# Two passes over the tokens in a kernel of pooled attention and a gated MLP, with Strassen's scheme in the second

## The chip, the cores and the metric

The kernel runs on one core of one Trainium2 chip. A core has five engines that run their own queues of instructions in order: TensorE (PE, matmuls and transposes; its weight loads are shown as PEld), VectorE (DVE), ScalarE (ACT), GpSimd (POOL) and SyncE (SP), which here issues all DMAs. Matmul results land in PSUM, in eight banks of 128 partitions x 512 fp32; everything else is worked on in SBUF. The metric is the device time of one execution in microseconds. Three runs of the kernel before gave 826.31, 827.72 and 828.11 us; the median is 827.72.

## The reference

Inputs are float32 q, k and v, and float64 weights (the kernel reads them as pairs of 32-bit words and makes fp32 numbers of them itself).

```python
# attention: q, k, v are (8 batches, 8 heads, 576 tokens, 64)
k_p = k.reshape(B, H, 72, 8, D).mean(axis=3)       # 8 neighbours pooled
v_p = v.reshape(B, H, 72, 8, D).mean(axis=3)
scores = (1 / sqrt(64)) * (q @ k_p.T)
attn = softmax(scores)                              # over the 72 pooled keys
x = (attn @ v_p) -> (4608 tokens, 512)
# MLP: w1, w2 (512, 1024), w3 (1024, 1024), w_out (1024, 512)
out = ((x @ w1) * (x @ w2)) @ w3 @ w_out            # (4608, 512)
```

## The kernel before

**Numbers.** Each matmul operand is split in two parts, hi + lo, of the type fp32r, and a product is made of three matmuls: hi*hi, hi*lo, lo*hi (`PASSES`, L499). `split` (L153) makes the parts: ACT casts to hi, DVE or POOL subtracts to get lo. A float64 weight becomes fp32 in four instructions: `high` on ACT (L133), `low` on DVE (L138), `conv_b` (L146) and `conv_c` (L150) on DVE.

**Start.** w3 @ w_out is computed once as W, since h @ w_out = g @ (w3 @ w_out). It takes 16 steps s (`w_mm`, L565): eight with the upper half of w3's rows (with w_out converted beside it by `w_block`, L166), eight with the lower half (`w_conv`, `w_conv2`, `w_conv3`, `w_split`, L214 to L227). Each step converts a 512 KB piece of w3, turns it by four PE transposes (`w_turn`, L207), splits it and runs 12 matmuls of 512 columns into four accumulators. `w_post` (L575) splits the result into W's tiles. Then, or beside it, 16 pieces of w1 and w2 are loaded, converted and split (`w12_conv` to `w12_split`, L229 to L248).

**Main loop.** The 4608 tokens go in 12 chunks m of 384. For each of the eight blocks j of 128 columns of w1 and w2, `a_mm` and `b_mm` (through `ab`, L503, matmul L510) compute 12 matmuls of 384 columns each; `a_post` copies a out of PSUM (ACT, L520), `b_post` multiplies (DVE, L530) and casts the product to hi (ACT, L531), `g_lo` makes lo (DVE, L536); `out_mm` (L538, matmul L545) runs nine matmuls of 512 columns (three token tiles, three passes) into `o0`, `o1`, `o2`, which collect over all j. `out_post` copies them out and stores them. The PSUM accumulators `a`, `b`, `o0`, `o1`, `o2` have one bank each.

**Attention** of chunk n is done while chunk n-1 is in the main loop, in three tiles of 128 tokens, or four of 96 where the chunk crosses a batch (n % 3 == 1). For each tile: scores in two halves of four heads (`s_mm`, L389), per half the row minimum, a subtraction, exp and a sum (`soft1`: DVE L405, L407, ACT L410, DVE L411; tiles in `SOFT_ACT` use another form, L415), normalisation (`soft2`, L424 to L427), the eight keys beyond 64 set aside in R (`soft3`, L436, L438), transposes (`pt_mm`, `ptr_mm`, L449, L459), their split (`pt_post`, L471, L472). Then four head pairs of probabilities times v (`av_mm`, L484 to L487), split into x (`av_post`, L495, L496). All attention results on PE share three PSUM buffers named `att`. k and v are pooled by additions on POOL (`pool_tree`, L346; three k pieces by DVE, L304, as listed in `K_DVE`); q is loaded in small pieces (L276) and transposed on DVE (L287).

**Order.** The order is written out by hand: `at(kind, k, fn, ...)` (L584) puts a step into slot k; steps are sorted by slot, within a slot by kind (L loads, P post-processing, M main matmuls, A attention matmuls), and each engine runs its part of that list in order. A main-loop chunk has 24 slots (3 per j): a, b, and at +5 the out group. K0 is the slot after the first eight w3 steps, M0 = K0 + 16 the slot where chunk 0 begins.

Of the kernel before, what the change touches and what calls it, by code (L numbers as in the profile page):

```python
# [29 lines left out]
):  # L30

    nc = tc.nc
# [14 lines left out]
    NK = DM // P  # L49
    CH = 384  # L50
    NCH = NTOK // CH

    SOFT_ACT = [(0, 0), (0, 1), (0, 2), (1, 1), (1, 2)]
    LO_DVE = [(0, 1), (4, 1), (6, 0)]
    K_DVE = [(0, 1), (1, 1), (1, 3)]
# [3 lines left out]
    xp = ctx.enter_context(tc.tile_pool(name="xp", bufs=2))  # L59
    p1 = ctx.enter_context(tc.tile_pool(name="p1", bufs=1))  # L60
    p2 = ctx.enter_context(tc.tile_pool(name="p2", bufs=2))
    stp = ctx.enter_context(tc.tile_pool(name="stp", bufs=4))
    osp = ctx.enter_context(tc.tile_pool(name="osp", bufs=3))
    pacc = ctx.enter_context(tc.tile_pool(name="pacc", bufs=1, space=PSUM))
    patt = ctx.enter_context(tc.tile_pool(name="patt", bufs=3, space=PSUM))


    ident = cp.tile([P, P], F32, name="ident")
    kbd = [cp.tile([P, NPR, 2 * KP], F32, name=f"kbd{i}") for i in range(2)]
    vbd = [[cp.tile([P, NPR, P], F32R, name=f"vbd{i}_{s}") for s in range(2)] for i in range(2)]  # L70
    VR = [cp.tile([P, NPR, P], F32R, name=f"VR{i}") for i in range(2)]
# [41 lines left out]
    def load_wo(j):  # L113
        raw["wo", j] = raw_cell(8 + j)
        nc.sync.dma_start(out=raw["wo", j], in_=wor[j * P:(j + 1) * P, :])

    def load_w3(s):
        h, j = divmod(s, NJ)
        raw["w3", s] = raw_cell(s % 4)
        nc.sync.dma_start(  # L120
            out=raw["w3", s].rearrange("p (i c) -> p i c", i=4),
            in_=w3r[h * 512:(h + 1) * 512, 2 * j * P:2 * (j + 1) * P].rearrange("(i p) c -> p i c", p=P))

    def load_w12(j, w):
# [19 lines left out]
    def conv_b(r, z):  # L144

        nc.vector.scalar_tensor_tensor(  # L146
            out=r, in0=z.bitcast(I32), scalar=3, in1=r, op0=ALU.logical_shift_left, op1=ALU.bitwise_or)

    def conv_c(r, z):
# [7 lines left out]
    def w_tiles(s):  # L157
# [4 lines left out]
        if s < NJ:  # L162
            stage["wo", s] = stage["wt"][s % 4], f(stage["wt"][4 + s % 3])
        stage["w3", s] = W_cell(0, 4 + s % 4, I32), W_cell(1, 4 + s % 4, F32)

    def w_block(v):  # L166
# [47 lines left out]
    def w_conv(s):  # L214
        w_tiles(s)
        conv_a(raw.pop(("w3", s)), *stage["w3", s])

    def w_conv2(s):
        conv_b(*stage["w3", s])

    def w_conv3(s):
        conv_c(*stage["w3", s])

    def w_split(s):
        ps = w_turn(s)
        w3t[s] = hl_cell(4 + s % 4)
        split(ps, *w3t[s])  # L227

    def w12_conv(j, w):  # L229
# [37 lines left out]
    def load_q(n, prs=range(NPR)):  # L267
        if ("q", n) not in stage:
            stage["q", n] = p1.tile([P, NPR, CH // 32, 32], F32, tag="qs", name="qs")
        t = stage["q", n]  # L270
        for pr in prs:
            for (b, s0, cnt, off) in pieces(n):
                for par in range(2):
                    for db in range(2):
                        g = 2 * par + db
                        nc.sync.dma_start(  # L276
                            out=t[32 * g:32 * g + 32, pr, off // 32:(off + cnt) // 32],
# [212 lines left out]
    def av_post(n, pr):  # L490
# [5 lines left out]
        nc.vector.tensor_tensor(out=xl, in0=ps, in1=f(xh), op=ALU.subtract)  # L496


    PASSES = ((0, 0), (0, 1), (1, 0))  # L499
# [38 lines left out]
    def out_mm(m, j):  # L538
# [3 lines left out]
        for t in range(3):  # L542
            c = slice(t * P, (t + 1) * P)
            for i, (sg, sw) in enumerate(PASSES):
                nc.tensor.matmul(out=oacc[m][t], lhsT=(gh, gl)[sg][:, c], rhs=W[j][sw],  # L545
# [189 lines left out]
```

## Time and profile before

| | us |
|---|---|
| median of three runs | 827.72 |
| profiled execution | 828.94 |
| its span, first to last instruction | 827.2 |
| PE busy | 784.6 |
| DVE busy | 460.5 |
| ACT busy | 283.2 |
| POOL busy | 205.7 |
| first main-loop matmul of chunk 0 starts | 107.74 |
| first main-loop matmul of chunk 1 starts | 184.03 |

The span is that of the profiled execution, which took 828.94 us as a whole. Busy times are sums of instruction durations; matmul ends are modelled and overlap the next start, so PE's pace is better read from starts. "Idle before" is the time an engine waited ahead of an instruction, with the instruction or transfer that ended the wait.

### The profile page before, as it was taken

What the parts mean: (1) busy time and instruction counts of PE and PEld (TensorE: products, weight loads), DVE (VectorE), ACT (ScalarE), POOL (GpSimd) and SP (SyncE); (2) the same over time, 40 slices, a digit from 0 to 9 for tenths busy, and PEclk for the clock granted to TensorE, in tenths of its full rate; (3) what the DMA queues carried; (4) which work ended last, traced back from release to release, by engine and by line L of the source; (5) the groups of instructions that cost most, each with busy time, mean ns of one, the idle gap of its engine ahead of it and who ended that gap; (6) DMA issues with size and microseconds to landing.
All of it is one profiled execution on the core that took longest, in us unless ns stands there. A gap on an engine that the chain in (4) does not pass through costs nothing.

```text
span 827.2 us, 11655 instructions
## 1 busy us (share of the span) xinstructions
PE 784.6 (95%) x4320; PEld 727.5 (88%) x4320; DVE 460.5 (56%) x921; ACT 283.2 (34%) x719; POOL 205.7 (25%) x234
## 2 busy tenths in 40 slices
PE   7877697799999999999999999999999999999998
PEld 6655596699999999999999999999999999999997
DVE  7987999937537436446345355365374374462112
ACT  4535555523224223323233234232243233232211
POOL 2152546601600811105104603006008112000000
PEclk8989988999999999999999999999999999999999
DMA  9996893005304402016014330053034030100101
GB/s 328 214 184 158 223 219 73 1 1 123 88 0 90 108 35 56 1 47 151 16 49 86 77 77 1 0 115 97 1 87 111 25 67 1 39 1 1 40 0 39
DMA packets 113161, 62.64 MB, mean 76 GB/s; under 512 B 80208, under 2 KB 96848, under 8 KB 113104
## 3 DMA queue, kind: packets, MB, share of 16 engines
q1 hardware_dynamic: 113104, 61.89, 30.2%
q8 instruction: 34, 0.56, 0.3%
q14 instruction: 23, 0.19, 0.1%
HBM read 52.43 MB, written 9.44 MB: 75 GB/s over the span
## 4 chain that ended last, share of the span: by engine, by line
PE 80%; DVE 10%; DMA 7%; issue 2%; ACT 1%; SPq 0%; DVEq 0%
PE a L510 23%; PE o L545 23%; PE b L510 23%; PE att L389 4%; DMA raw<-in_moe_w_dram 3%; PE att L449 2%; DMA qs<-in_q_dram 2%; PE att L486 1%; PE att L484 1%; PE att L485 1%; PE att L487 1%; DMA raw<-in_moe_w_out_dram 1%; DVE wb L146 1%; PE att L459 1%; DVE wb L138 1%
## 5 line engine op out<-in xcount | busy, mean ns | idle before, releaser
L510 PE MATMUL a<-xT,hl 128*128 128x384 f32 x1152 | 224.1, 343 | 0.0
L510 PE MATMUL b<-xT,hl 128*128 128x384 f32 x1152 | 221.4, 340 | 0.0
L510 PEld LDWEIGHTS a<-xT,hl 128*128 128x128 f32 x1152 | 206.4, 192 | 4.8
L510 PEld LDWEIGHTS b<-xT,hl 128*128 128x128 f32 x1152 | 200.0, 189 | 0.0
L545 PE MATMUL o<-Wc,gh 128*128 128x512 f32 x576 | 183.6, 400 | 0.0
L530 DVE TENSOR_TENSOR a<-b,a 128x384 f32<-128x384 f32 x96 | 53.1, 554 | 125.8 <-PE b L510 125.7
L545 PEld LDWEIGHTS o<-Wc,gh 128*128 128x128 f32 x576 | 105.1, 189 | 17.3
L347 POOL TENSOR_TENSOR st<-st 72x512 f32<-72x512 f32 (+1 forms) x53 | 75.0, 1415 | 175.2 <-DMA st<-in_k_dram 162.4
L545 PE MATMUL o<-Wc,gl 128*128 128x512 f32 x288 | 114.0, 396 | 0.0
L520 ACT COPY a<-a 128x384 f32<-128x384 f32 x96 | 45.9, 479 | 182.8 <-PE a L510 163.6
L531 ACT CAST gh<-a 128x384 fp32r<-128x384 f32 x96 | 49.2, 512 | 149.0 <-DVE a L530 149.0
L536 DVE TENSOR_TENSOR gl<-a,gh 128x384 fp32r<-128x384 f32 x96 | 62.4, 650 | 34.9 <-ACT gh L531 34.5
L360 POOL TENSOR_TENSOR vbd<-vm,vbd 64x256 fp32r<-64x256 f32 x16 | 13.4, 836 | 253.2 <-ACT vbd L359 248.3
L496 DVE TENSOR_TENSOR xT<-att,xT 128x384 fp32r<-128x384 f32 x48 | 26.6, 556 | 70.8 <-ACT xT L495 70.8
L545 PEld LDWEIGHTS o<-Wc,gl 128*128 128x128 f32 x288 | 54.1, 188 | 12.5
L411 DVE TENSOR_REDUCE sm<-E 128x4 f32<-128x288 f32 (+1 forms) x70 | 31.6, 451 | 46.3 <-ACT E L410 46.3
L571 PE MATMUL o<-hl 128*128 128x512 f32 x144 | 45.3, 455 | 11.0 <-DVE hl L179 10.9
L389 PE MATMUL att<-kbd,qT 128*128 128x144 f32 (+1 forms) x320 | 53.3, 290 | 2.0 <-ACT E L415 2.0
L405 DVE TENSOR_REDUCE mx<-att 128x4 f32<-128x288 f32 (+1 forms) x80 | 35.9, 449 | 29.5 <-PE att L389 29.5
L389 PEld LDWEIGHTS att<-kbd,qT 128*128 128x128 f32 (+1 forms) x320 | 47.4, 182 | 3.1 <-ACT E L415 2.5
L410 ACT ACTIVATE E<-E 128x288 f32<-128x288 f32 (+1 forms) x70 | 31.1, 445 | 55.1 <-DVE E L407 55.1
L571 PEld LDWEIGHTS o<-hl 128*128 128x128 f32 x144 | 30.3, 218 | 19.3 <-DVE hl L179 12.9
(87 smaller groups left out, 850.1 us busy)
## 6 DMA issues: line engine op xcount, KB each, us to landing
raw<-in_moe_w_dram SPq DMA_DIRECT2D x32, 512.0 KB
st<-in_k_dram SPq DMA_DIRECT2D x32, 288.0 KB
out_dram<-ob SPq DMA_DIRECT2D x35, 256.0 KB
st<-in_v_dram SPq DMA_DIRECT2D x32, 256.0 KB
qs<-in_q_dram SPq DMA_DIRECT2D x128, 48.0 KB
raw<-in_moe_w_out_dram SPq DMA_DIRECT2D x8, 512.0 KB
st<-in_v_dram SPq DMA_DIRECT2D x64, 64.0 KB
qs<-in_q_dram SPq DMA_DIRECT2D x128, 24.0 KB
```

Of the source, the lines that this page charges most:

```text
L347: nc.gpsimd.tensor_tensor(out=t[:, :, 0:4], in0=t[:, :, 0:4], in1=t[:, :, 4:8], op=ALU.add)
L389: nc.tensor.matmul(out=ps[:nt, 2 * KP * j:2 * KP * (j + 1)], lhsT=qT[n][:, pr, off:off + nt], rhs=kbd[b % 2][:, pr], start=True, stop=True,)
L405: nc.vector.tensor_reduce(out=mx[:nt, hs], in_=sv, axis=AX.X, op=ALU.min)
L410: nc.scalar.activation(out=E[:nt, hs], in_=E[:nt, hs], func=AF.Exp, scale=-1.0)
L411: nc.vector.reduce_sum(out=sm[:nt, hs], in_=E[:nt, hs], axis=AX.X)
L510: nc.tensor.matmul(out=o, lhsT=w12[j, w][sw][:, kt * P:(kt + 1) * P], rhs=x[sx][:, kt], start=(i == 0), stop=(i == 3 * NK - 1))
L520: nc.scalar.copy(out=a, in_=gt[m, j][:, :CH])
L530: nc.vector.tensor_tensor(out=g, in0=ps[:, :CH], in1=g, op=ALU.mult)
L531: nc.scalar.copy(out=gh, in_=g)
L536: nc.vector.tensor_tensor(out=gl, in0=g, in1=f(gh), op=ALU.subtract)
L545: nc.tensor.matmul(out=oacc[m][t], lhsT=(gh, gl)[sg][:, c], rhs=W[j][sw], start=(j == 0 and i == 0), stop=(j == NJ - 1 and i == 2))
L571: nc.tensor.matmul(out=wacc[h][it], lhsT=w3t[s][sa][:, it * P:(it + 1) * P], rhs=wo[j][sb], start=(j == 0 and i == 0), stop=(j == NJ - 1 a ...
```

## The change

The tokens are gone through twice. The first pass is the old loop with four of the eight blocks j (`NA = 4`), so it uses half of w1's and w2's columns and half of W. Its result goes to a scratch tensor in DRAM (`pd`), and x goes there too (`xd`). In the first pass's slots the second half of W is computed in eight units, one a chunk (`w2_load` to `w2_post`), and stored (`wbd`); from chunk 8 on the other half of w1 and w2 is converted, and the sums that Strassen's scheme needs are made and split (`w12b_*`).

The second pass goes through the eight batches of 576 tokens. For each of four groups qq (two of w1, two of w2, each 256 columns by 512 rows), the product of 2 x 2 blocks is made of seven block products instead of eight (Winograd's form): six matmuls of 288 columns each, in one of five accumulators in turn. The sums of x are made once a batch, the sums of the products by DVE adds from PSUM; for w2 POOL multiplies with the w1 result. Then tiles of 128 tokens go through the second half of W, the first pass's partial result is loaded and added, and the sum is stored.

In the start, the w3 steps are eight instead of 16, and the w1/w2 pieces eight instead of 16; M0 is K0 + 8. A chunk has 12 slots. One piece of k goes from DVE to POOL (`K_DVE`), two lo parts of w1/w2 too (`LO_DVE`), q is buffered per head pair, `stp` and `osp` have one buffer less, `out_post` always copies on ACT, and the SBUF pools of the first pass are released for those of the second.

```diff
-    LO_DVE = [(0, 1), (4, 1), (6, 0)]
-    K_DVE = [(0, 1), (1, 1), (1, 3)]
+    LO_DVE = [(0, 1)]
+    K_DVE = [(0, 1), (1, 1)]
...
+    def w2_conv(u):
+        t = cell(11, [P, 2, 512], I32, "wt")
+        stage["w2", u] = t[:, 0], f(t[:, 1])
+        conv_a(raw.pop(("w2", u)), *stage["w2", u])
...
+    def w2_mm(u):
+        ps = stage["w2p", u] = patt.tile([P, 512], F32, tag="att", name="att")
+        t = w3t.pop(("w2", u))
+        for jj in range(4):
+            for i, (sa, sb) in enumerate(PASSES):
+                nc.tensor.matmul(out=ps, lhsT=t[sa][:, jj * P:(jj + 1) * P], rhs=wo[4 * (u % 2) + jj][sb],
+                                 start=(jj == 0 and i == 0), stop=(jj == 3 and i == 2))
...
+    def w12b_sums(qq):
+
+        r0, r1 = (f(stage["vr"][:, jj]) for jj in range(2))
+        a11, a12, a21, a22 = r0[:, :256], r0[:, 256:], r1[:, :256], r1[:, 256:]
+        t = stage["vz"]
+        s1, s2, s3, s4 = (t[:, i, 256 * o:256 * o + 256] for i in range(2) for o in range(2))
+        add(s1, a21, a22)
+        sub(s2, s1, a11)
+        sub(s3, a11, a21)
+        sub(s4, a12, s2)
...
         nc.scalar.copy(out=xh, in_=ps)
-        nc.vector.tensor_tensor(out=xl, in0=ps, in1=f(xh), op=ALU.subtract)
+        sub(xl, ps, f(xh))
+        if n == pr == 0:
+            stage["xs"] = cell(13, [P, 2, CH], F32, "xs")
+        x = stage["xs"][:, pr % 2]
+        nc.scalar.copy(out=x, in_=ps)
+        for (b, s0, cnt, off) in pieces(n):
+            nc.sync.dma_start(out=xd[b][:, pr, s0:s0 + cnt], in_=x[:, off:off + cnt])
...
+    GROUPS = (("A11", "B11"), ("S2", "T2"), ("S1", "T1"), ("S3", "T3"),
+              ("A12", "B21"), ("S4", "B22"), ("A22", "T4"))
...
+    def x_split(i, n):
+        t = (r1, l1)[i % 2]["p"].tile([P, 2, 2, HS], F32R, tag=f"xo{XN.index(n)}", name="xo")
...
+        split(src, *xo[i, n])
...
+    def grp_mm(i, qq, n):
+        wn, xn = GROUPS[n]
+        ps = acc[i, qq, n] = pacc.tile(
+            [P, 512], F32, tag=("a", "b", "o0", "o1", "o2")[(28 * i + 7 * qq + n) % 5], name="ps")
+        w, x = sw[qq, wn], xo[i, xn]
+        for j, (kt, (a, b)) in enumerate((kt, p) for kt in range(2) for p in PASSES):
+            nc.tensor.matmul(out=ps[:, :HS], lhsT=w[a][:, kt * P:(kt + 1) * P], rhs=x[b][:, kt],
+                             start=(j == 0), stop=(j == 5))
+
+    def grp_post(i, qq, n):
...
+            if w2:
+                add(tmp[into], u, o)
+                nc.gpsimd.tensor_tensor(out=d, in0=d, in1=tmp[into], op=ALU.mult)
+            else:
+                add(d, u, o)
...
+            nc.scalar.copy(out=tmp["m1"], in_=o)
+        elif n == 1:
+            add(tmp["u2"], tmp["m1"], o)
...
+    def out2_mm(i, t, half):
...
+                nc.tensor.matmul(
+                    out=oacc["b", no], lhsT=G[no][a][:, j], rhs=W[1, j][b],
+                    start=(j == 0 and n == 0), stop=(j == 3 and n == 2))
...
+        add(ob, part.pop(no), oacc.pop(("b", no)))
+        nc.sync.dma_start(out=out[no * P:(no + 1) * P], in_=ob)
...
-    M0 = F0 + 2 * NS
+    M0 = K0 + 8
+    IA = 3 * NA
+    E0 = M0 + IA * NCH
+    B0 = E0 + 3
+    IB = 25
...
     for n in range(1, NCH):
-        k = M0 + 3 * NJ * (n - 1)
+        k = M0 + IA * (n - 1)
         nt = len(tok_tiles(n))
-        s0, pt, av = (3, 5.5, 20.5) if n == 1 else (0, 6, 17) if nt == 4 else (0, 5, 15)
...
+        plan_att(n, k, *(
+            ([-4, -2, 0, 2], [0, 2, 5, 7], [8, 8.5, 9, 9.5]) if n == 1 else
+            ([-7, -4, -1, 2], [-2, 1, 4, 7], [8, 8.5, 9, 9.5]) if nt == 4 else
+            ([-7, -3, 1], [-2, 2, 6], [7, 8, 8.5, 9])))
...
+        for g in range(28):
+            k = k0 + g / 2 + (0 if g < 7 else 10.5)
+            at("M", k, grp_mm, i, *divmod(g, 7))
+            at("P", k // 1 + 1 + 0.02 * (k % 1), grp_post, i, *divmod(g, 7))
+        x0 = k0 - (12 if i == 0 else 20)
+        at("L", x0 - 3 if i else x0, x_load, i)
...
+            at("M", r0 + 2 * t + h, out2_mm, i, t, h)
```

More of the change, by code (lines that the diff above doesn't have):

```diff
@@ L212, in w_turn, with w12a_conv @@
         return ps
[L214 to L229, printed above, removed]
+    def w12a_conv(j, w):
         i = 2 * j + w
@@ new lines, in w2_post, with load_w12b @@
+    def w2_post(u):
+        it, hf = divmod(u, 2)
+        ps = stage.pop(("w2p", u))
+        if hf == 0:
+            stage["w2s"] = cell(10, [P, 512], F32, "ws")
+            nc.scalar.copy(out=stage["w2s"], in_=ps)
+        else:
+            add(stage["w2s"], stage["w2s"], ps)
+            nc.sync.dma_start(out=wbd[it], in_=stage["w2s"])
+    NAMES = ("A11", "A12", "S1", "S2", "S3", "S4", "A22")
+    OWN = ((0, 1, 2), (3, 4, 5), (6, 7, 8), (9, 10, 11))
+    BOTH = (12, 13)
+    sw = {}
+    def load_w12b(qq, jj):
+        raw["w12b", qq, jj] = (
+            cell(9, [P, 1024], I32, "raw") if qq < 3 else wcell(jj, [P, 1024], I32, "raw"))
+        load_w12(raw["w12b", qq, jj], NA + 2 * (qq // 2) + jj, qq % 2)
@@ new lines, in w12b_split @@
+    def w12b_split(qq, i):
+        src = stage["sums", qq][i]
+        if i < 3:
+            t = cell(OWN[qq][i], [P, 2, 512], F32R, "sw")
+            for o in range(2):
+                c = slice(256 * o, 256 * o + 256)
+                sw[qq, NAMES[2 * i + o]] = t[:, 0, c], t[:, 1, c]
+            split(src, t[:, 0], t[:, 1])
+            return
+        if qq % 2 == 0:
+            stage["both"] = cell(BOTH[qq // 2], [P, 2, 2, 256], F32R, "sw")
+        both = stage["both"][:, :, qq % 2]
+        sw[qq, "A22"] = both[:, 0], both[:, 1]
+        split(src, *sw[qq, "A22"])
@@ L571, in w_mm @@
                 nc.tensor.matmul(
-                    out=wacc[h][it], lhsT=w3t[s][sa][:, it * P:(it + 1) * P], rhs=wo[j][sb],
-                    start=(j == 0 and i == 0), stop=(j == NJ - 1 and i == 2))
-    def w_post(h):
-        for it in range(4):
-            i = 4 * h + it
-            W[i] = [W_cell(x, i, F32R) for x in range(2)]
-            split(wacc[h][it], *W[i])
+                    out=wacc[0][it], lhsT=w3t[s][sa][:, it * P:(it + 1) * P], rhs=wo[s][sb],
+                    start=(s == 0 and i == 0), stop=(s == NJ - 1 and i == 2))
@@ new lines, with xb, x_load, x_sum1 @@
+    XN = ("B11", "T2", "T1", "T3", "B21", "B22", "T4")
+    GROUPS = (("A11", "B11"), ("S2", "T2"), ("S1", "T1"), ("S3", "T3"),
+              ("A12", "B21"), ("S4", "B22"), ("A22", "T4"))
+    x32, xo, acc, tmp, G, part = {}, {}, {}, {}, {}, {}
+    def xb(i, k2, t2):
+        return x32[i][:, 2 * k2:2 * k2 + 2, t2 * HS:(t2 + 1) * HS]
+    def x_load(i):
+        x32[i] = r2["x"].tile([P, NK, S], F32, tag="x32", name="x32")
+        nc.sync.dma_start(out=x32[i], in_=xd[i])
+    def x_sum1(i):
+        t = stage["xs", i] = [r2["x"].tile([P, 2, HS], F32, tag="xs", name="xs") for _ in range(2)]
+        sub(t[0], xb(i, 0, 1), xb(i, 0, 0))
+        sub(t[1], xb(i, 1, 1), t[0])
@@ new lines, in g_rest @@
+    def g_rest(i, odd):
+        no = 9 * (i // 2) + 4
+        if not odd:
+            G[no] = [l1["p"].tile([P, 4, P], F32R, tag=tag, name=tag) for tag in ("ghs", "gls")]
+        for p in range(2):
+            split(G[i, p][:, :, :64] if odd else G[i, p][:, :, S - 64:],
+                  *(x[:, 2 * p:2 * p + 2, 64 * odd:64 * odd + 64] for x in G[no]))
+    def out2_mm(i, t, half):
+        no, _ = out_tiles(i)[t]
+        if half == 0:
+            oacc["b", no] = patt.tile([P, 512], F32, tag="att", name="att")
+        for j in (2 * half, 2 * half + 1):
+            for n, (a, b) in enumerate(PASSES):
+                nc.tensor.matmul(
+                    out=oacc["b", no], lhsT=G[no][a][:, j], rhs=W[1, j][b],
+                    start=(j == 0 and n == 0), stop=(j == 3 and n == 2))
```

379 lines of the change are left out of this document (245 added, 134 removed).

## The prediction

> **What bounds the kernel now.** I read the page first (span, busy times, the slices and the chain), then busy time by stage, then single instructions of PE and DVE in order of time, then the groups by shape.
>
> ```profile
> span 827.2 us, 11655 instructions
> PE 784.6 (95%) x4320; PEld 727.5 (88%) x4320; DVE 460.5 (56%) x921; ACT 283.2 (34%) x719; POOL 205.7 (25%) x234
> PE   7877697799999999999999999999999999999998
> DVE  7987999937537436446345355365374374462112
> PE 80%; DVE 10%; DMA 7%; issue 2%; ACT 1%; SPq 0%; DVEq 0%
> ```
>
> The slices show two regimes: up to about slice 8 (165 us) DVE is full and PE has holes; after it PE is full and DVE is at half. The stages, cut where chunk 0 and chunk 1 start (columns: stage, its length, busy us and count of PE, PEld, DVE, ACT, POOL, clock, DMA share, GB/s):
>
> ```profile
> 0.00:107.70 107.70, 79.72 (x366) 64.68 (x367) 92.37 (x156) 51.76 (x135) 36.21 (x45) 0.88 0.87 227
> 107.70:184.00 76.30, 65.63 (x348) 60.90 (x347) 62.02 (x104) 35.56 (x104) 38.72 (x27) 0.91 0.30 60
> 184.00:823.20 639.20, 639.20 (x3609) 601.90 (x3608) 305.66 (x661) 195.55 (x480) 130.73 (x162) 1.00 0.21 51
> ```
>
> From 184.0 us on PE has no idle time at all. So there the time is the sum of PE's instructions, and only fewer or shorter matmuls help; before it, only less DVE work does. PE's pace comes from starts, since ends are modelled:
>
> ```profile
> 184.03 2.27 PE L510 MATMUL a<-xT,hl 128*128 128x384 f32 x12
> 228.71 2.24 PE L510 MATMUL a<-xT,hl 128*128 128x384 f32 x12
> 230.79 0.34 PE L484 MATMUL att<-PTh,vbd 128*128 128x384 f32 x1
> 233.57 0.62 PE L545 MATMUL o<-Wc,gh 128*128 128x512 f32 x2
> 235.66 2.27 PE L510 MATMUL a<-xT,hl 128*128 128x384 f32 x12
> 242.27 1.92 PE L510 MATMUL a<-xT,hl 128*128 128x384 f32 x10
> 347.17 0.25 PE L484 MATMUL att<-PTh,vbd 128*128 128x192 f32 x1
> 348.03 2.27 PE L510 MATMUL b<-xT,hl 128*128 128x384 f32 x12
> 819.04 4.19 PE o L545 x18
> ```
>
> Twelve matmuls of 384 columns take 230.79-228.71 = 2.08 us, 0.1733 each; the nine of 512 (three tiles, three passes) 235.66-233.57 = 2.09, 0.2322 each. Both are 0.451 to 0.454 ns a column, with no fixed part. The eight of 192 columns take 348.03-347.17 = 0.86, 0.1075 each, not 0.0867: a floor. A chunk takes 242.27-184.03 = 58.24 us. Of it 192 x 0.1733 + 72 x 0.2322 = 50.0 are MLP matmuls, 8.25 attention. Check: 184.0 + 10 chunks x 58.24 + one without attention 50.0 + the two out groups left over from chunk 0 (4.2) = 820.6; PE ends at 823.2. The span is 4.0 longer (last copy and store), the execution 828.94, so 1.7 lie around the span.
>
> **The change, part by part.**
>
> *PE after the start.* A first-pass chunk has 96 x 0.1733 + 36 x 0.2322 = 25.0 us of MLP and keeps its 8.25 of attention: 33.25. The second half of w3 @ w_out, which leaves the start, becomes 96 matmuls of 512 columns (22.3) and 32 transposes, at the floor of 0.1075 (3.4). The second pass has 8 x 28 x 6 = 1344 matmuls of 288 columns and 36 x 12 = 432 of 512. A matmul of 288 columns is not in the trace. Its bounds are the floor, 0.1075, and the 384-column row, 0.1733; since 288 x 0.451 = 0.130 lies above the floor I take 0.130, for 174.7 us, plus 100.3. From the start of chunk 1: 10 x 33.25 + 25.0 + 4.2 + 25.7 + 275.0 = 662.4. The same stretch in the kernel before is 636.7. So Strassen's seven products for eight save 1152 x 0.1733 - 174.7 = 25 us, and the moved w3 half takes 25.7 of it back. On PE alone the steady part wins nothing. What can be won lies before chunk 1.
>
> [...]
>
> *The start.* Before chunk 1 DVE is the limit: 92.4 + 62.0 = 154.4 us in 184. What leaves it is priced by these groups (columns: count, busy us, mean ns, idle before):
>
> ```profile
> L150 DVE SCALAR_TENSOR_TENSOR Wc<-Wc 128x512 int32<-128x512 int32 x16 | 13.8, 863 | 0.3
> L146 DVE SCALAR_TENSOR_TENSOR Wc<-Wc 128x512 int32<-128x512 int32 x16 | 11.7, 731 | 0.1
> L138 DVE TENSOR_SCALAR Wc<-raw 128x512 int32<-128x512 int32 x16 | 8.2, 521 | 2.9 <-DMA raw<-in_moe_w_dram 2.9
> L155 DVE TENSOR_TENSOR hl<-att,hl 128x512 fp32r<-128x512 f32 x8 | 5.4, 679 | 7.1 <-ACT hl L154 7.1
> L155 DVE TENSOR_TENSOR Wc<-o,Wc 128x512 fp32r<-128x512 f32 x6 | 3.8, 678 | 0.0
> L146 DVE SCALAR_TENSOR_TENSOR wb<-wb 128x512 int32<-128x512 int32 x16 | 13.6, 848 | 0.2 <-ACT wb L133 0.2
> L150 DVE SCALAR_TENSOR_TENSOR wb<-wb 128x512 int32<-128x512 int32 x16 | 11.1, 693 | 0.0
> L138 DVE TENSOR_SCALAR wb<-raw 128x512 int32<-128x512 int32 x16 | 11.9, 742 | 0.0
> L304 DVE TENSOR_REDUCE km<-st 72x128 f32<-72x1024 f32 x3 | 5.7, 1910 | 0.0
> ```
>
> Half of the w3 conversions (33.7 / 2) and all eight L155 splits (5.4) go: 22.3. Four splits of the combined W: 4 x 0.68 = 2.7. Half of the w1/w2 conversions: 36.6 / 2 = 18.3. One L304 goes to POOL: 1.9. Four of chunk 0's eight j, at 0.554 + 0.659 (rows below): 4.9. Together 50.1. Against it, attention of chunk 2 now begins in chunk 0, about half a chunk's softmax, 9 us (19.1 a chunk, below). DVE's work before chunk 1 becomes 113 us. At the occupancy of the start so far (92.4 of 107.7 = 0.86) that is 132 us, with no idle time but the first 4 us or so it is 118. I take 124, nearer the lower end, since the idle time late in the kernel before's chunk 0 came from PE's queue of work, which halves; 118 to 136 stay for the range. DMA doesn't bind earlier: 227 GB/s x 107.7 us = 24.4 MB before chunk 0; 16 loads of 512 KB fewer leave 16 MB, 71 us, and by the same DVE sum chunk 0 starts near 82.
>
> *The first pass.* DVE's rows from 184 to 823 us:
>
> ```profile
> L536 DVE TENSOR_TENSOR gl<-a,gh 128x384 fp32r<-128x384 f32 x88 | 58.0, 659 | 33.7 <-ACT gh L531 33.4
> L530 DVE TENSOR_TENSOR a<-b,a 128x384 f32<-128x384 f32 x88 | 48.8, 554 | 120.9 <-PE b L510 120.9
> L407 DVE TENSOR_TENSOR E<-att,mx 128x288 f32<-128x288 f32 x42 | 19.2, 457 | 1.4
> L411 DVE TENSOR_REDUCE sm<-E 128x4 f32<-128x288 f32 x42 | 19.0, 453 | 21.5 <-ACT E L410 21.5
> L472 DVE TENSOR_TENSOR PTl<-att,PTh 128x512 fp32r<-128x512 f32 x21 | 14.5, 690 | 10.0 <-ACT PTh L471 10.0
> L411 DVE TENSOR_REDUCE sm<-E 96x4 f32<-96x288 f32 x24 | 10.8, 449 | 22.7 <-ACT E L410 22.7
> L557 DVE COPY ob<-o 128x512 f32<-128x512 f32 x12 | 8.2, 683 | 1.7 <-PE o L545 1.7
> L472 DVE TENSOR_TENSOR PTl<-att,PTh 128x384 fp32r<-128x384 f32 x12 | 6.6, 554 | 10.7 <-ACT PTh L471 10.7
> ```
>
> Without the MLP rows (106.8) and the copies (8.2, which go to ACT) 190.7 of 305.66 us are attention: 19.1 a chunk. With four j (4.9) and a w3 unit (one conversion at the means above, 2.1, a split 0.68, half an add) that is 27 us. Added to it are waits inside the softmax which stay as long as the order of its steps does: (21.5 + 22.7 + 10.0 + 10.7) / 10 = 6.5 a chunk. So DVE needs 33.5 us where PE needs 33.25 + 3.2 = 36.4, 92% of the time; before, the same sum was some 36 of 58. Two in-order engines so close, coupled by three "att" buffers, will stall each other. Chunk 9 is worse: no w3 unit, but Strassen's weights, each of four groups 2 x (0.85 + 0.69 + 0.74) + 3 splits x 0.68 + five short ones, about 8.7 us; one and a quarter fall in it: 19.1 + 4.9 + 10.9 + 6.5 = 41 against 33, 8 us late. Bounds for all stalls of the pass: 4 (chunk 9, partly caught up) and 40 (every chunk at 39.5). I take 14.
>
> ACT gains the copies of x (48, near 0.5 us) and all stores' copies and stays near 60%. The stores of x add four to eight DMAs a chunk to SP's queue, each behind an ACT copy; the loads of q, k, v queued behind them run 2.6 slots (7 us) ahead of POOL, which hides that. It costs if SP is full:
>
> ```profile
> 252.15 11.65 SPq L276 DMA_DIRECT2D qs<-in_q_dram x24
> ```
>
> At 0.49 us an issue, some 41 issues a chunk are 20 us of 36. Covered.
>
> *The second pass.* For one of eight batches PE has 28 x 6 x 0.130 + 4.5 x 12 x 0.2322 = 34.4 us. DVE has 28 adds at 0.457 (12.8), four sums and seven splits of twice that size (at most 10.1), ten G splits (4.1), 4.5 last adds at 0.69 (3.1): 30 by durations, which overlap in the trace (L407 lasts 0.46, and so on). PE stays ahead as long as five accumulators, 3.9 us of work, cover DVE's bursts. Bounds of the stalls: 0 and 25 (3 a batch); I take 6, nearer the covered side. The join of the passes waits for three ACT copies of chunk 11's accumulators, which the second pass's third to fifth groups reuse; in the 6.
>
> *The end.* After the last product PE waits for its add, the G split, then runs five tiles: 3 us more than before, 7 in all beyond PE's sum.
>
> *Sum.* 124 + 662.4 + 14 + 6 + 7 = 813.4 span, + 1.7 = 815.1 against 828.94 of the profiled execution. That execution is 1.2 above the median of 827.72, so I state **814**.
>
> **The rivals.**
>
> *DVE sets the first pass (slower).* Its price is above: 92% is a mean, and POOL's blocking grows with density:
>
> ```profile
> 382.80 1.44 DVE L536 TENSOR_TENSOR gl<-a,gh 128x384 fp32r<-128x384 f32 x1
> ```
>
> beside the mean of 0.659. If DVE's chunk comes to 38.6 with that and with imperfect order, eight chunks lose 2.2 and chunk 9 and its neighbours 18: 36 instead of 14, **836**. The point: stalls of the pass above 27 us. [...]
>
> *Nothing stalls.* The start takes 118, the first pass loses 4, the second 2: **794**. For it: 92% and 87% are below 100. Against: 15% of DVE idle in the start.
>
> *The second pass follows DVE.* Should the adds wait behind splits that wait for ACT, 3 us a batch: 24 instead of 6, **832**. Against it: the adds depend on PE alone.
>
> [...]
>
> **How the numbers follow.** Forecast 802 to 825: 0.43. Nothing stalls: 0.21. DVE sets the first pass: 0.24. Second pass on DVE: 0.08. Exposed loads: 0.02. More mishaps at once, beyond 850: 0.02. A measurement of this kernel can tell about 0.2% (1.7 us) from no change. Faster than 826.1: 0.43 + 0.21 + 0.03 from the lighter cases of the others = 0.67; within: 0.05; slower: 0.28. The range 790 to 845 leaves out some 0.04 below and 0.12 above.
>
> **What would show it.** Chunk 1 starting at 118 to 136 us; first-pass chunks of 36 to 38 us with PE idle ended by DVE and ACT of the softmax, most in chunk 9; a group of six 288-column matmuls every 0.78 us; PE idle in the second pass below 1 us a batch. Wrong would be a pace at 288 columns off 0.130, first-pass chunks of 39 us or more, or DVE busy throughout the second pass.

## The result, and the profile after

The changed kernel takes 960.91 us (median of four runs, 958.3 to 964.29) beside 827.91 for the kernel before on the same chip: 1.1611 times as long, 95% interval 1.1571 to 1.1652. The forecast was 814, its upper end 845. The profiled execution took 958.3 us. From its page:

```profile
span 956.2 us, 13006 instructions
...
PE 796.3 (83%) x4512; PEld 725.4 (76%) x4512; DVE 624.6 (65%) x1273; ACT 336.8 (35%) x863; POOL 244.5 (26%) x295
...
PE   7633679694989594989695978998899999999998
...
DVE  7948667454686463576564677747776776686644
...
PEclk8875689797999797999798999999899999999999
...
PE 42%; DVE 23%; DMA 13%; ACT 9%; SPq 6%; issue 5%; POOL 2%; DVEq 0%; ACTq 0%; POOLq 0%
```

PE is busy 12 us longer than before (796.3 against 784.6), so nearly all of the loss is idle time of PE. Its slices are ragged from slice 1 to slice 28 (about 24 to 690 us), not only in the start, and wherever PE is at 6 tenths or less the granted clock is at 8 or less. DVE is not full anywhere after the start. The stages, cut at the first matmul of chunk 0, of chunk 1 and of the second pass (columns as before):

```profile
0.00:108.86 108.86, 61.52 (x259) 48.05 (x260) 83.53 (x138) 47.39 (x135) 46.62 (x54) 0.73 0.77 188
108.86:160.79 51.93, 41.56 (x219) 37.84 (x219) 33.03 (x68) 22.78 (x76) 25.17 (x30) 0.88 0.31 80
160.79:665.47 504.68, 411.53 (x2262) 377.79 (x2261) 308.85 (x648) 197.04 (x487) 119.38 (x147) 0.92 0.36 98
665.47:956.20 290.73, 281.74 (x1777) 261.69 (x1775) 199.20 (x421) 69.55 (x167) 53.32 (x64) 0.99 0.29 97
```

| | forecast | measured | difference |
|---|---|---|---|
| chunk 1 starts at | 124 | 160.8 | +36.8 |
| rest of the first pass | 387.4 + 14 = 401.4 | 504.7 | +103.3 |
| second pass and end | 288 | 290.7 | +2.7 |

The second pass does what was forecast. In the first, PE is idle for 504.68 - 411.53 = 93.2 us where 14 were forecast, and its instructions last 411.5 - 387.4 = 24.1 longer. Which waits these are, the list of waits of the stretch from 160.79 to 665.47 us says (engine and operation that waited, what released it: us in total, times, longest):

```profile
PE att L407 <- ACT PTr L570: 65.7, 6, 12.9
...
SPq L596 <- ACT vbd L453: 74.2, 6, 19.8
SPq L650 <- ACT ob L649: 64.9, 14, 17.9
...
SPq L596 <- ACT R L530: 39.5, 9, 18.0
SPq L596 <- ACT xs L594: 31.7, 15, 6.3
...
SPq L650 <- ACT R L530: 8.2, 3, 3.6
```

Six waits of 11 us each make 65.7 of PE's 93.2. PE stands before the transposes of the pooled k (L407), which need a buffer of `att` that ACT's copy of PTr is to set free. SP, which issues all DMAs in order, stands for 145.4 us before stores of x (L596) and 73.1 before stores of a chunk's result (L650), since ACT has not written what they send. One such hole in order of time, in the timelines of SP, ACT and PE:

```profile
357.22 0.54 SPq L596 DMA_DIRECT2D xd<-xs  x1
357.80 7.77 SPq L370 DMA_DIRECT2D qs<-in_q_dram  x16
365.67 5.39 SPq L435 DMA_DIRECT2D st<-in_v_dram  x8
371.10 3.83 SPq L370 DMA_DIRECT2D qs<-in_q_dram  x8
375.04 3.13 SPq L650 DMA_DIRECT2D pd<-ob  x3
...
362.40 1.06 ACT L649 COPY ob<-o 128x512 f32<-128x512 f32 x2
377.24 0.59 ACT L649 COPY ob<-o 128x512 f32<-128x512 f32 x1 [13.78 <-DMA pd<-ob]
...
357.83 2.25 PE L609 MATMUL b<-xT,hl 128*128 128x384 f32 x12
359.91 0.65 PE L483 MATMUL att<-kbd,qT 128*128 128x144 f32 x4
...
378.73 0.71 PE L407 MATMUL att<-ident,km 72*128 72x72 f32 x4 [12.86 <-ACT PTr L570]
379.24 1.06 PE L236 MATMUL att<-ident,wt 128*128 128x128 f32 x4
379.95 4.19 PE L609 MATMUL b<-xT,hl 128*128 128x384 f32 x12
383.94 0.79 PE L644 MATMUL o<-W,gh 128*128 128x512 f32 x2
```

At 362.40 ACT copies two of chunk 4's three results into the two `ob` buffers. Their stores stand in SP's queue behind 24 loads of q and 8 of v's remainder, 17 us of issuing (0.49 and 0.67 each), and go out from 375.04 on. ACT waits 13.78 us for a buffer for the third copy, with the copies PTh and PTr queued behind it, and PE waits for PTr. It is a ring of in-order queues: SP, ACT, PE. All six holes look like this one: SP issues 22 or 32 loads in a row right ahead of the stores, for 12.4 to 18.4 us, and ACT waits 10.2 to 13.8 us for a buffer. Up to the stores SP does not stand still; it issues. (In three of the six the stores then take another 5 us to free the buffer, here 2.) And the hole has a second price: the next twelve matmuls of b take 383.94 - 379.95 = 3.99 us, and 359.91 - 357.83 = 2.08 before it. The windows around it show why (columns as in the stages; PE's clock is the third number from the end):

```profile
340.00:363.50 23.50, 22.33 (x129) 20.80 (x128) 16.38 (x35) 11.51 (x28) 13.46 (x18) 1.00 0.50 126
363.50:378.70 15.20, 2.37 (x15) 2.05 (x13) 1.74 (x4) 1.35 (x3) 2.83 (x4) 0.73 0.35 93
378.70:390.00 11.30, 11.27 (x49) 10.38 (x50) 7.97 (x19) 4.65 (x13) 0.00 (x0) 0.75 0.06 23
390.00:400.00 10.00, 10.00 (x61) 9.60 (x60) 5.47 (x11) 4.64 (x12) 1.73 (x2) 1.00 0.14 42
```

Cut finer, the granted clock is 1.00 up to 370 us, 0.66 from 370 to 372, 0.50 up to 384, 0.86 from 384 to 385 and 1.00 from there on: it fell some 4.8 us after PE went idle (365.87) and came back some 5.6 us after PE started again (378.73). Under the clock of 0.50 the twelve matmuls took 3.99 / 2.08 = 1.9 times as long.

### The profile page after: what moved, and what is told of

Its sections match the earlier page's. It is cut to its first block, busy times and chain, and to the rows that moved or that the text cites. A ratio compares the mean times of both kernels' runs of the same rounds, so it can differ in the third digit from the quotient of the medians.

```text
span 956.2 us, 13006 instructions
## 1 busy us (share of the span) xinstructions
PE 796.3 (83%) x4512; PEld 725.4 (76%) x4512; DVE 624.6 (65%) x1273; ACT 336.8 (35%) x863; POOL 244.5 (26%) x295
## 4 chain that ended last, share of the span: by engine, by line
PE 42%; DVE 23%; DMA 13%; ACT 9%; SPq 6%; issue 5%; POOL 2%; DVEq 0%; ACTq 0%; POOLq 0%
PE ps L730 18%; PE att L797 10%; DMA st<-in_v_dram 4%; DMA pd<-ob 4%; PE b L609 4%; SPq L370 3%; PE o L644 3%; SPq L435 3%; PE a L609 3%; DMA raw<-in_moe_w_dram 2%; PE att L284 2%; DVE E L501 2%; DVE xT L126 2%; ACT E L504 2%; DVE E L521 2%
## 5 line engine op out<-in xcount | busy, mean ns | idle before, releaser
L730 PE MATMUL ps<-xo,sw 128*128 128x288 f32 x1344 | 182.2, 297 | 4.4 <-ACT m L749 4.4
L730 PEld LDWEIGHTS ps<-xo,sw 128*128 128x128 f32 x1344 | 181.5, 190 | 5.3 <-ACT m L749 4.6
L609 PE MATMUL b<-xT,hl 128*128 128x384 f32 x576 | 123.6, 367 | 2.1 <-DVE a L629 2.1
L609 PE MATMUL a<-xT,hl 128*128 128x384 f32 x576 | 115.1, 349 | 4.5 <-ACT xT L589 2.6
L609 PEld LDWEIGHTS b<-xT,hl 128*128 128x128 f32 x576 | 111.0, 209 | 2.6 <-DVE a L629 2.4
L609 PEld LDWEIGHTS a<-xT,hl 128*128 128x128 f32 x576 | 104.4, 195 | 7.4 <-ACT xT L589 2.9
L644 PE MATMUL o<-W,gh 128*128 128x512 f32 x288 | 93.5, 406 | 0.7 <-ACT ob L649 0.7
L797 PE MATMUL att<-W,gh 128*128 128x512 f32 x256 | 80.2, 394 | 0.0
L407 PE MATMUL att<-ident,km 72*128 72x72 f32 x32 | 5.7, 321 | 68.8 <-ACT PTr L570 65.7
L644 PEld LDWEIGHTS o<-W,gh 128*128 128x128 f32 x288 | 53.0, 192 | 9.6 <-ACT ob L649 1.2
L407 PEld LDWEIGHTS att<-ident,km 72*128 72x128 f32 x32 | 4.2, 206 | 71.3 <-issue 38.6
L644 PE MATMUL o<-W,gl 128*128 128x512 f32 x144 | 57.3, 398 | 0.1
```

Of the source, the lines that this page charges most:

```text
L609: nc.tensor.matmul(out=o, lhsT=w12[j, w][sw][:, kt * P:(kt + 1) * P], rhs=x[sx][:, kt], start=(i == 0), stop=(i == 3 * NK - 1))
L730: nc.tensor.matmul(out=ps[:, :HS], lhsT=w[a][:, kt * P:(kt + 1) * P], rhs=x[b][:, kt], start=(j == 0), stop=(j == 5))
L797: nc.tensor.matmul(out=oacc["b", no], lhsT=G[no][a][:, j], rhs=W[1, j][b], start=(j == 0 and n == 0), stop=(j == 3 and n == 2))
```

## The experiments

Four theories for the first pass. **Q**: loads and stores share SP's queue, so stores go out late and ACT blocks. **B**: two `ob` buffers are too few. **D**, the prediction's rival: softmax on DVE and ACT sets the pace. **S**: Strassen's scheme costs more than forecast. Ratios are to the kernel before, with 95% intervals.

**e1, e2, e3: stores issued by ACT.** ACT makes the data, so a store on its own queue has no other engine to wait for; SP stood 218.5 us at these stores. e1 moves the first of these two, e2 the second, e3 both.

```diff
-        nc.sync.dma_start(out=pd[3 * m + t], in_=ob)
+        nc.scalar.dma_start(out=pd[3 * m + t], in_=ob)
...
-            nc.sync.dma_start(out=xd[b][:, pr, s0:s0 + cnt], in_=x[:, off:off + cnt])
+            nc.scalar.dma_start(out=xd[b][:, pr, s0:s0 + cnt], in_=x[:, off:off + cnt])
```

> Only edit: the stores of the first pass's result (pd) are issued by ACT right behind the copy, instead of by SP. Theory Q (SP's in-order queue): ACT's third copy of a chunk waits for one of two ob buffers, whose store stands in SP's queue behind q and v loads; 84.8 us of ACT's time went there and PE's kt transposes waited 65.7 us behind it. Then those waits fall to under 25 us and the time falls to 870 to 900. Theory D (DVE and its softmax waits set the first pass, the rival of the prediction): ACT's wait only shows that the pass is late anyway; the time stays within 15 us of 960.

> Only edit: the stores of x (xd) are issued by ACT behind the copy instead of by SP; the pd stores stay on SP. Theory Q: SP stood some 170 us at these stores, waiting for ACT; loads and pd stores behind them come earlier, but 24 q and 8 v issues (17 us) still stand ahead of the pd stores, so only part returns: 910 to 945. Theory D: within 15 us of 960.

> Both edits: xd and pd stores on ACT, SP keeps loads and nothing that waits for ACT in the first pass but wbd. Theory Q: no store is left in the way; first-pass chunks fall from 49 us to about 40 and the time to 840 to 875, with DVE then the nearest limit. Theory D: within 15 us of 960.

Measured: e1 953.53 us (1.1524, 1.1495 to 1.1552), e2 932.43 (1.1269, 1.1243 to 1.1295), e3 932.91 (1.1267, 1.1239 to 1.1295). e1 missed Q's range widely and lies where D said. In the list of waits over the whole changed kernel stands (us in total, times, longest)

```profile
ACT ob L649 <- DMA pd<-ob: 84.8, 12, 13.8
```

and in that of e1:

```profile
ACT vrh L460 <- POOL vrm L443: 57.0, 8, 10.0
...
ACT ob L649 <- DMA pd<-ob: 19.9, 11, 5.8
```

The wait for `ob` fell from 84.8 us in all to 19.9, but ACT now stood 57 us before the cast of v's remainder: the loads are late too, since SP stands at the stores of x (155.5 us in its list). The wait moved; it was not removed. Taking the stores of x off SP (e2) is worth 28 us, as Q said. Both together (e3) give no more, where Q said 840 to 875: ACT still waits for `ob`, now behind stores that go out at once, as e3's list says:

```profile
ACT ob L649 <- DMA pd<-ob: 26.7, 12, 5.7
```

So two buffers don't cover the three transfers here.

**e4, e5, e6: the buffers.** e4 takes one `ob` buffer from the kernel before. e5 puts the third result of a chunk into a free cell of SBUF; e6 is e5 with the stores of x from ACT.

```diff
     def out_post(m, t):
-        ob = osp.tile([P, DM], F32, tag="ob", name="ob")
+        if t == 2 and m <= 8:
+            ob = cell(12, [P, DM], F32, "ob")
+        else:
+            ob = osp.tile([P, DM], F32, tag="ob", name="ob")
```

> The kernel before with two output buffers instead of three, as the change has. Theory Q: no change (within 0.5%), since SP's queue is empty when the stores come (SP waited 454 us for ACT there), so that a buffer comes back in 2 us. If two buffers alone are the cost, ACT stalls in every chunk and 11 chunks lose 2 us or more each: 850 or more.

> Only edit: the third copy of a chunk's result goes to a cell that is free at that time, so that it waits for no store. In the first run, where ACT issued the pd stores, the wait at the copy had only moved on to the vrh copy (57 us, for v's remainder loaded late). Theory Q (loads late in SP's queue; the wait shows at whichever instruction ACT reaches first): 945 to 960 again, with ACT's wait at the copy gone and waits at vrh or vbd grown. Theory B (the buffer is the cause): below 900.

> Third buffer as in e5, and the stores of x on ACT. In the third run 26.7 us were left at the copy (store in flight on ACT's own queue) with PE's clock falling after each. Theory Q: chunks that begin a batch fall from 46 to 48 us to 40 to 43; 895 to 920. Theory D (softmax and DVE set the first pass): within 10 us of 932.

Measured: e4 828.95 (1.0016, 1.0002 to 1.0031), e5 937.71 (1.1332, 1.1288 to 1.1375), e6 917.26 (1.1087, 1.1032 to 1.1141). The kernel before doesn't need the third buffer; the changed one gains 23 us from it, neither what B said nor what Q said, and 44 with the stores of x moved. e6 lies in Q's range, but not by Q's sign: the chunks that were to fall to 40 to 43 us still take 45 to 47. Buffers and queue are two ways to loosen one ring; neither alone is the cause.

**e7, e8: fewer issues.** One DMA with rows of 1.5 KB brings a whole q tile in place of four or eight, so q's values stand in other places than the reference's. e8 adds e6's edits.

```diff
-                for par in range(2):
-                    for db in range(2):
...
+            nc.sync.dma_start(
+                out=t.rearrange("p n e -> p (n e)"),
+                in_=q[pieces(n)[0][0]].rearrange("h s d -> (h s d)")[49152 * pr:49152 * (pr + 1)].rearrange(
+                    "(p e) -> p e", p=P))
```

> Each of the 48 q tiles is filled by one DMA of 128 rows of 1.5 KB instead of four or eight of 128-byte pieces (q's values are then others than the reference's). Everything else as in the changed kernel, the stores on SP included. Theory Q in full (SP's issues are what makes loads late): 256 issues fall to 48, some 90 us of SP's time; first-pass chunks fall below 44 us and the start gets shorter too: 860 to 900. If SP's waits for ACT at the stores matter more than its issues: 925 to 950. Theory D: within 15 us of 960.

> All three: one DMA per q tile (q's values differ), third buffer, x stored from ACT. Theory Q: nothing on SP is late any more; what is left in the first pass is the softmax and DVE, 38 to 41 us a chunk, and the start no longer waits for DMAs of 128-byte pieces: 835 to 870. Theory D: above 920.

Measured: e7 901.32 (1.0892, 1.0855 to 1.093), e8 897.32 (1.0848, 1.0815 to 1.0882). The largest single gain, 60 us, just outside Q's range, and with it the other edits bring only 4 more, so e8 misses Q's 835 to 870. The lists of waits of e7 in its first pass (162.33 to 610.41 us; its L402 is the changed kernel's L407, L645 its L650, L591 its L596) say which part of SP's queue mattered:

```profile
PE att L402 <- ACT PTr L565: 10.2, 4, 4.2
...
ACT ob L644 <- DMA pd<-ob: 31.2, 10, 5.6
...
SPq L645 <- ACT ob L644: 92.9, 19, 17.9
SPq L591 <- ACT vbd L448: 71.3, 6, 17.8
...
SPq L591 <- ACT R L525: 40.9, 9, 17.5
SPq L591 <- ACT xs L589: 34.4, 19, 6.2
...
SPq L645 <- ACT R L525: 6.3, 3, 2.1
```

SP stands at the stores as long as before, 245.8 us against 218.5, and yet PE's wait before the transposes of k falls from 65.7 to 10.2 us, and ACT's for `ob` in the same stretch from 83.3 to 31.2. So the burst of issues ahead of the stores made the holes, more than SP's standing at them. The edit also makes the rows of the loads longer, and no run shows what that alone does to their transfers; but in the hole shown above the DMA engines were busy only 0.35 of the time, while SP issued without a pause. The windows of e8, start and first pass:

```profile
0.00:107.64 107.64, 61.59 (x258) 48.32 (x259) 84.73 (x138) 47.05 (x133) 44.98 (x54) 0.73 0.68 197
164.56:606.32 441.76, 403.05 (x2262) 367.69 (x2261) 299.50 (x649) 197.85 (x487) 109.21 (x139) 0.98 0.35 108
```

The first pass fell by 504.7 - 441.8 = 62.9 us, in idle time of PE (93.2 to 38.7) and in clock (0.92 to 0.98, PE's busy time 411.5 to 403.1). The start didn't move (107.6 against 108.9), although Q had said that it would get shorter: its loss is another matter. And 441.8 is still 40 above forecast, so Q isn't all.

**e9, e10, e11: a short softmax.** No row minimum is taken and nothing subtracted; ACT makes exp straight from PSUM, DVE only sums. e10 adds e6's edits, e11 e8's (with q's values in other places).

```diff
-        nc.vector.tensor_reduce(out=mx[:nt, hs], in_=sv, axis=AX.X, op=ALU.min)
-        if (n, t) not in SOFT_ACT:
-            nc.vector.tensor_tensor(
-                out=E[:nt, hs], in0=sv,
-                in1=mx[:nt, hs].unsqueeze(2).broadcast_to([nt, 4, KP]), op=ALU.subtract)
-            nc.scalar.activation(out=E[:nt, hs], in_=E[:nt, hs], func=AF.Exp, scale=-1.0)
-            nc.vector.reduce_sum(out=sm[:nt, hs], in_=E[:nt, hs], axis=AX.X)
-            return
+        nc.scalar.activation(out=E[:nt, hs], in_=sv, func=AF.Exp, scale=-1.0)
+        nc.vector.reduce_sum(out=sm[:nt, hs], in_=E[:nt, hs], axis=AX.X)
+        return
```

> The changed kernel with a shorter softmax for all tiles: exp straight from PSUM, without the row minimum and its subtraction (the quotient is the same). DVE loses two instructions of 0.46 us per half tile, some 6.5 us a chunk, and each half's chain loses two hops. Theory Q (late loads on SP alone): PE's holes stay where they are, 945 to 960. Theory D (softmax and DVE set first pass and start): the start shortens by 10 us or more and chunks by 5: below 900.

> The same short softmax on the kernel with the third buffer and x stored from ACT (917). If both theories hold a part, loads come in time more often and DVE is no longer near PE: 870 to 895. Theory Q alone: 905 to 920.

> The short softmax on the kernel with one DMA per q tile, third buffer and x stored from ACT (897; q's values differ). If late loads and the softmax are the two causes of what the first pass loses, PE now runs at its own sum there, 387 to 400 us from chunk 1 to the second pass, and the start falls towards 140: 820 to 850. If a third cause is left: above 865.

Measured: e9 925.57 (1.1194, 1.1167 to 1.1221), e10 870.0 (1.0536, 1.0496 to 1.0576), e11 854.96 (1.0343, 1.032 to 1.0366). e9 gains 35 us, between what Q and D said: both causes are there. The softmax's share is of the same size with the ring loosened: e6 to e10 47 us, e8 to e11 42, of which 32 lie in the first pass both times and most of the rest in the start. e11 lies between its two ranges. The first pass of e11:

```profile
151.50:560.76 409.26, 391.04 (x2263) 361.63 (x2261) 242.72 (x523) 194.16 (x486) 108.81 (x139) 1.00 0.38 116
```

It is 8 us above the 401.4 forecast, at full clock, with 18.2 us of PE idle. So 63 of the 103 us lost in the first pass come back with the short loads and the loosened ring and 32 more with the short softmax, in that order.

**e12: Strassen's price.** One of the seven products of each group is computed twice, so 192 matmuls of 288 columns are added. The second time starts the accumulator anew, so the result stays the same.

```diff
-        for j, (kt, (a, b)) in enumerate((kt, p) for kt in range(2) for p in PASSES):
+        for rep in range(2 if n == 6 else 1):
+            for j, (kt, (a, b)) in enumerate((kt, p) for kt in range(2) for p in PASSES):
```

> The changed kernel with the last of Strassen's seven products run twice, so that the second pass has eight groups of six matmuls per 2 x 2 block product, as without the scheme. If the second pass is PE's sum at 0.130 us a matmul, 192 matmuls more cost 25.0 us: 984 to 988. If weight loads were exposed at 288 columns, 192 x 0.238 = 46 us: above 1000. If DVE set the second pass, less than 10 us.

Measured: 984.56 (1.1906, 1.1876 to 1.1936), 23.65 above the changed kernel, 0.123 a matmul. Its windows from the second pass on:

```profile
670.00:985.10 315.10, 307.24 (x1969) 287.17 (x1967) 200.10 (x421) 69.16 (x167) 53.70 (x64) 0.99 0.26 90
```

315.1 against 290.7: the whole addition stands in this stage. The pace can also be read straight from starts, in the changed kernel at a granted clock of 1.00:

```profile
711.36 22.48 PE L730 MATMUL ps<-xo,sw 128*128 128x288 f32 x168
733.67 0.63 PE L797 MATMUL att<-W,ghs 128*128 128x512 f32 x2
```

That is (733.67 - 711.36) / 168 = 0.133 us. The difference of the medians is a looser measure, since executions of one kernel here lie 5 to 6 us apart. S is out; the second pass is PE's own sum, and an eighth product costs about what the forecast said. (The 0.238 in the expectation is 0.130 and, for a load, the 0.1075 that a matmul of 192 columns took; no run shows an exposed load.)

**e13, e14: the start.** The timelines of ACT, DVE and PE in the changed kernel:

```profile
54.00 0.32 ACT L509 ACTIVATE E<-att,mx 128x72 f32<-128x72 f32 x1 [1.60 <-DVE mx L499]
...
60.79 0.30 ACT L460 CAST vrh<-vrm 128x128 fp32r<-128x128 f32 x1 [4.91 <-POOL vrm L443]
...
61.72 0.30 ACT L509 ACTIVATE E<-att,mx 128x72 f32<-128x72 f32 x1
...
64.36 0.69 DVE L182 TENSOR_TENSOR W<-o,W 128x512 fp32r<-128x512 f32 x1 [6.69 <-ACT W L181]
...
66.89 1.09 PE L543 MATMUL att<-ident,E 128*128 128x128 f32 x4 [9.18 <-DVE E L521]
```

The row minima of the first attention tile's two halves were there by 56 us (L499 ran at 53.51 and 55.39). ACT made the first half's exponentials from 54.00 us on, but the second half's only from 61.72 on, because a cast that needs the last load of v stood ahead of them in its queue. (The first expectation below takes 61.72 for the first exponential of all.) e13 puts that cast and POOL's sum behind the exponentials; e14 does so in e11.

```diff
-        at("P", load + d * 6 + lag, prep_vr, b)
+        at("P", load + d * 6 + lag + (4.5 if b == 0 else 3 if b == 1 else 0), prep_vr, b)
...
-    plan_kv(0, K0 - 14.5, 1.5, 4, K0 - 4, K0 - 0.5, K0 + 1)
+    plan_kv(0, K0 - 14.5, 1.5, 4, K0 - 4, K0 - 0.5, K0 + 4.5)
...
-            plan_kv(b, K0 - 3.5, 1.75, 3, M0 - 4, k + 2, k + 3)
+            plan_kv(b, K0 - 3.5, 1.75, 3, M0 - 4, k + 2, k + 6)
```

> The changed kernel, with the steps on the remainder of v of batches 0 and 1 (ACT's cast of it and POOL's last additions) 4.5 and 3 slots later, so that on ACT's queue they stand behind the first exponentials. Theory A (the start is late because ACT, whose queue is in order, waits 4.91 us at 60.79 us for POOL's sum of a load of v, with the ready exponentials of the first attention tile behind it): the first exponential comes at 54 to 57 us instead of 61.72, chunk 0 starts 3 to 7 us earlier than 108.9, chunk 1 3 to 10 us earlier than 160.8, and the median falls by as much, to 951 to 958. Theory D (the chain DVE to ACT to DVE to PE of seven attention tiles with no MLP matmul beside it sets the start, whatever waits in it): chunk 0 within 2 us of 108.9, median 959 to 963.

> The same two steps later, on top of the short softmax, one DMA for each q tile, the third buffer and the stores of x from ACT (854.96 us without; q's values differ, no row minimum is taken). Theory A: chunk 0 starts at 93 to 97 instead of 99.8, chunk 1 at 142 to 148 instead of 151.5, median 845 to 851. Theory D: chunk 1 within 2 us of 151.5, median 853 to 857. In neither case is it as fast as the kernel before, since the first pass stays at about 409 us against 387 for PE alone.

Measured: e13 952.62 (1.1504, 1.1482 to 1.1527), e14 848.97 (1.0267, 1.0245 to 1.029), 8 and 6 us less, the medians that A named. The stages moved less: chunk 0 starts at 107.55 in e13 and 98.33 in e14, where A said at most 105.9 and 97 and D, for e13, within 2 us of 108.9; chunk 1 at 155.8, as A said, and 148.5, just outside. The profiled execution of e13 is the longest of its four, 958.5, and e12, whose start is the changed kernel's, has chunk 1 at 164.6, so a stage of a single execution is good to some 4 us. In e13 ACT no longer waits for POOL there. The second half's exponentials come at 59.37, 2.35 us earlier; the first half's come at 57.49, where A said 54 to 57 and 54.00 was the time without the edit, since their minimum was ready only then (L499 ran at 57.00).
So this wait is one link of the start's chain, worth 5 of the 37 us at chunk 1 in e13 and 3 in e14; the short softmax is worth 13.1 (e8 to e11) and 19.5 (e6 to e10). What holds the rest is open: PE's waits there are mostly of a few us, the longest 9.2, each for a step of attention's chain from DVE to ACT and back, with no MLP matmul to run beside it, but no run took that chain away.

**e15: the short softmax in the kernel before** (the diff of e9).

> The kernel before with the short softmax alone (no row minimum and no subtraction, all row sums on DVE). If a long softmax costs time only where PE waits for it, the kernel before gains only ahead of 184 us, where DVE loses minima of 6.1 and subtractions of 1.8 us and gains ten sums at 0.45: 1 to 6 us, 822 to 827, and PE has no idle time after chunk 1 starts, as before. If the softmax costs time in the steady part also (by PE's accumulators or the att buffers), it gains a good part of the 32 us that the changed kernel gained from it: under 815.

Measured: 821.92 us (six runs) against 827.54: 0.9943, 0.9921 to 0.9965. It is 0.6% faster than the kernel before, just below the 822 to 827 expected. Its windows:

```profile
0.00:102.31 102.31, 80.07 (x367) 65.89 (x368) 90.62 (x156) 46.93 (x93) 38.80 (x45) 0.87 0.89 232
102.31:177.41 75.10, 63.30 (x348) 57.77 (x347) 59.53 (x96) 31.46 (x76) 38.26 (x27) 0.95 0.31 70
177.41:816.00 638.59, 638.59 (x3608) 601.71 (x3606) 248.10 (x529) 187.83 (x480) 130.61 (x162) 1.00 0.21 51
```

Chunk 1 starts 6.6 us earlier (184.0 to 177.4). After it DVE has 57.6 us less work (305.7 to 248.1) and PE's stretch is the same length (639.2 and 638.6). The same edit that gives the changed kernel's first pass some 32 us gives this one's steady part nothing: beside a chunk of 58 us the softmax is covered, beside one of 36 it is not. Without the row minimum, scores of large size could overflow exp; the minimum itself cancels in the quotient.

No version of the change that was run beats the kernel before; the best that computes the reference's function is e10 with 870.0. A fourth buffer for loads of k and v was not tried, nor were other slots for the units of w3 or for the start's attention.

## Why the prediction was wrong

- **PE's sum: right, in part by balance.** Second pass and end took 290.7 us for 288: PE's own time is 281.7 for 275.0, and its idle time 9.0 for 13, so two small errors cancel. A matmul of 288 columns, not in the trace of before, was taken at 0.130 us; it measures 0.133 from starts, and e12 gives 0.123 by the medians and (315.1 - 290.7) / 192 = 0.127 by the stage, the same within the spread. e12 has no room for a weight load on top: 23.65 us were measured, where matmuls with exposed loads, at the expectation's 0.238 each, would have taken 46. Strassen's saving on PE is real (23.7 us by the medians, 25 forecast). The chance of 0.02 given to exposed loads rests on no run, and exposed loads would be paid by all 1344 of these matmuls, not by the 192 of e12 alone.
- **"The second pass follows DVE": did not occur.** PE is busy 281.7 of 290.7 us.
- **"Covered", of SP's queue: the step that failed.** The prediction multiplied some 41 issues by 0.49 us, found 20 us of 36, and let the loads' lead of 7 us hide the stores' ACT copies. That is a mean over a chunk, and the order inside it decides: 22 or 32 issues in a row, 12.4 to 18.4 us, stand ahead of the stores of a chunk's result, and ACT waits 10.2 to 13.8 us behind them for one of two `ob` buffers. The fence that was read for 0.49 (24 loads, 11.65 us) was also the length for which a store behind them waits. The third `ob` buffer that the change takes away was not priced at all. SP also stands at each store until ACT has written its data, 145.4 + 73.1 = 218.5 us in the first pass, which the prediction did not count either; taking the larger part of that away brings 28 us (e2). With short loads alone 57 of the first pass's 103 us come back (504.7 to 448.1, e7), and 63 with the ring loosened too (e8).
- **The first pass's stalls: mis-sized.** 14, at most 40, were forecast; 93.2 us idle were measured, and 24.1 of longer instructions at a mean clock of 0.92, for which the forecast had no term. DVE is busy 308.9 of 504.7 us, 61%, and in only 23 of PE's 93 idle ones, so its load was not the limit there. The rival "DVE sets the first pass" (36 us of stalls) comes into its own once the ring is loosened: e8 is left with 38.7 us of idle time, DVE is busy in 27 of them, and chunk 9, which the prediction had named, is the longest chunk with 47.0 us. The blocking by POOL that this rival names is seen at g's lo part (L536, in the changed kernel L635): POOL ran an addition (L347) from 382.54 us on, for 1.28, beside the row of 1.44, and of the 88 such instructions after 184 us the 64 with no POOL instruction beside them took 0.553 us in the mean, the 24 others 0.947. In the changed first pass it is 0.543 in 33 and 1.331 in 12, and the mean of all rose from 0.659 to 0.753. The short softmax takes 32 us out of that pass (e8 to e11). It takes 56.8 us of work off DVE and shortens the chain DVE, ACT, DVE at once, so no run tells the load from the length of the chain. Of e8's 38.7 us 13.9 are waits of PE for the copies of x that the change adds on ACT; no run takes those away.
- **The start: work right, occupancy wrong.** DVE's work before chunk 1 was forecast at 113 us and is 83.53 + 33.03 = 116.6. It was spread over 160.8 us, an occupancy of 0.73 where 0.91 was taken, for the reason that idle time came from PE's queue, "which halves". Of DVE's 44 us of idle time there, 34 ended with ACT and only 4 with PE. That the w3 steps which are gone had filled such waits before is likely, but no run shows it. Chunk 0 starts where it did before (108.9 and 107.7), not near 82.

## What to carry to other kernels

When a change moves a store into a queue that also carries loads, price the longest run of issues that can stand ahead of the store, and the buffers that must cover it, not only the queue's mean use; price the time that the queue stands at the store too, and look for the ring: buffer, store, queue, load, engine, buffer. When the work that covers a chain across engines is made shorter, compare the chain's length with the new period, and not the engines' busy shares alone: with DVE busy 299.5 of 441.8 us (e8) a shorter softmax was still worth 32 us. An edit that shortens such a chain is worth most where nothing covers it, here in the start of the old kernel (e15: 6.6 us before chunk 1, nothing after it).

## What the runs showed of the hardware

The idle gap of 12.9 us at 366 us cost PE twice: after it the granted clock stood at half for another 5.6 us (12 matmuls of 384 columns in 3.99 us, not 2.08). Over the first pass PE's instructions lasted 24.1 us longer than forecast at a mean clock of 0.92, in e8 15.7 at 0.98 and in e11 3.6 at 1.00. Half of PE's busy time under the half clock, which is what the clock accounts for, is 19.0, 6.3 and 0.0 us of these; the rest is not explained, except that the forecast's own check of the kernel before had come out 2.6 us short (820.6 for 823.2). Matmuls of 288 columns with a new weight load each (1344 of both) ran at 0.133 us at a granted clock of 1.00, close to the 0.130 that a pace of 0.451 ns a column gives. The 0.1075 us of a matmul of 192 columns, which the prediction calls a floor, is not one: four of 144 columns took 0.39 us in the kernel before (188.72 to 189.11 us), 0.0975 each. Ahead of the hole at 366 us one DMA issue took 0.49 (q) or 0.67 us (v) of SP's time (16 in 7.77 us, 8 in 5.39), and the 32 in a row held the stores behind them for 17.2 us (357.80 to 375.04).
